# Retention and low-rank mixer on one Trainium2 core: w1 and w2 issued between the last casts of v, batches 1 to 3 loaded in 1.5 MB transfers and turned by PE (batch 1) or DMA (2, 3), retention in 64-row tiles

## Chip, cores and metric

The kernel runs on one core of a Trainium2 chip. Its engines are TensorE (PE, matrix products, with a queue of its own for weight loads, PEld), VectorE (DVE), ScalarE (ACT), GpSimd (POOL) and SyncE (SP, which only issues transfers). The metric is the device time of one execution in microseconds (us), as a median of several runs. A profile shows one execution; its span reaches from the first to the last instruction.

## What is computed

```python
def _attn_ref(q, k, v):                     # each (4, 8, 768, 64)
    gamma = 1.0 - 2.0 ** (-5.0 - np.arange(H))
    scale = 1.0 / np.sqrt(D)
    for t in range(S):
        state = gamma * state + einsum('bhd,bhe->bhde', k[:, :, t], v[:, :, t])
        y[:, :, t] = scale * einsum('bhd,bhde->bhe', q[:, :, t], state)

def _moe_ref(x, U, V, w_ch1, w_ch2):        # x: y as (4, 768, 512); U (768, 32), V (32, 768)
    h = x.transpose(0, 2, 1) @ U @ V        # w_ch1 (512, 2048), w_ch2 (2048, 512)
    u = x + h.transpose(0, 2, 1)
    return u + np.maximum(u @ w_ch1, 0.0) @ w_ch2
```

Retention with a decaying state per head is followed by a low-rank mixing along the sequence and by an MLP over the channels. Inputs and output are float32; the kernel works in bfloat16 with float32 sums.

## The kernel before

The recurrence is worked in chunks of 128 positions, six per batch. The decay is folded into q and v by factors (gqT, gk). For each chunk PE forms the scores k times q for all heads (`score4`), DVE multiplies them with a causal mask, and PE adds the masked scores times v and q times the running state (`mix4`); the state gathers k times v (`state`). The result x is mixed (`lr_proj`, `lr_expand`), the sum u is turned (`lr_turn`, by PE for batches 0 and 1, by DMA transposes on SP for 2 and 3), and the MLP makes up products with w1 (line L438), their ReLU into gT (ACT L445, DVE L443) and down products with w2 (L461), to which DVE adds u (L468).

All instructions are written out in a fixed order; no scheduler moves them, and each engine runs its own in that order. Batch 0's retention comes first, by functions of its own (`cast_early`, `turn_early`, `score_early`, `state_early`, `mix_early`). Then `weave` lays the MLP of batch b - 1, as a list of pieces with costs, and puts the retention of batch b between the pieces: each mark is a fraction of the total cost and a function, and the function is called ahead of the first piece that begins at or behind its mark. 56 pieces make up a stretch of cost 41.47; a large piece (0.864) is four products of 512 columns. The marks come from AT and LR, with one set for batch 1 and one for batches 2 and 3.

Loads of batches 1 to 3 go by SP. k and q are loaded whole, into four strips of 32 partitions, two heads in each, with runs of 1 KB (`load_whole`, L111), v (and for batches 2 and 3 a second, natural copy of k) in pieces of 256 KB with runs of 256 B (L130) into a ring of 19 buffers; `feed_more` issues them as buffers come free. POOL casts a chunk (`prep_turned`, `prep_natural`, lines L83 and L85), DVE turns k and q with its stream transpose (`turn_chunk`, L284), and retention works in 32-row tiles. For batch 1, natural k is won back by PE from the turned one (`natural_k`, L296). q, k and v of batch 0 are loaded ahead of all else by `load_early`.

The weights are loaded by POOL, which casts on the way: U, V, then w1 in four parts behind the last cast of v of batch 0, and w2 in four parts among the casts of batch 1. A one-element copy, `gate`, waits for the end of the first part of w1 and holds back the loads of batch 1:

```python
    for mb in range(4):
        load_w1(mb)
    gate = rinT.tile([P, 2, NCK, 256], fp32, tag="kin", name="gate")
    nc.gpsimd.tensor_copy(out=gate[:1, 0, 0, :1], in_=w1b[:1, NCB - 1, 511:512])
```

PSUM holds two tiles R of two banks each, for scores, mixing and turning, three banks "mlp" and one for the state. The output sums have three buffers (`o_sb`); their stores go out on POOL's queue (L427), but the last.

Of the kernel before, what the change touches and what calls it, by code (L numbers as in the profile page):

```python
# [16 lines left out]
def kernel(  # L17
# [21 lines left out]
    RING = 19  # L39
# [52 lines left out]
    feed = []  # L92
    n_fed, n_used, n_held = [0], [0], [0]
    ready = {}
    turned_in = {}
    n_cast = {b: 0 for b in range(-1, B)}

    def feed_natural(nm, b, ci):
        src = {"k": k, "v": v}[nm]
        feed.append(((nm, b, ci),  # L100
                     src[b, :, ts(ci, P), :].rearrange("h p d -> p h d")))

    def open_in(nm, b):
        turned_in[nm, b] = rinT.tile([P, 2, NCK, 256], fp32, tag=nm + "in",
                                     name=f"{nm}in_{b}")

    def load_whole(nm, b):
        open_in(nm, b)
        src = {"q": q, "k": k}[nm][b]
        for hp in (0, 2, 1, 3):  # L110
            nc.sync.dma_start(  # L111
                out=turned_in[nm, b][ds(32 * hp, 32)].rearrange(
                    "p h c x -> p (h c) x"),
                in_=src[ds(2 * hp, 2)].rearrange("h (c t j) d -> t (h c) (j d)",
                                                 c=NCK, t=32))

    def feed_more():
        while n_fed[0] < len(feed) and n_held[0] < RING:
            key, src = feed[n_fed[0]]
            if key[0] == "T" and n_cast[key[1] - 1] < 2 * NCK:  # L120
                return
            n_fed[0] += 1
            if key[0] == "T":
                load_whole("k", key[1])
                load_whole("q", key[1])
                continue
            n_held[0] += 1
            t = rin.tile([P, 512], fp32, tag="in", name=f"in_{n_fed[0]}")
            ready[key] = t
            nc.sync.dma_start(out=t.rearrange("p (h d) -> p h d", h=H), in_=src)  # L130

    def take(*key):
        n_held[0] -= 1
        return ready.pop(key)

    for b in range(1, B):
        feed.append((("T", b), None))
        for ci in range(NCK):
            if b > 1:
                feed_natural("k", b, ci)  # L140
            feed_natural("v", b, ci)
    NB = S // 256
    early = {}
    kin0 = rinT.tile([P, NB, H, P], fp32, tag="kin", name="kin_0")
    qin0 = rinT.tile([P, NB, H, P], fp32, tag="qin", name="qin_0")

    def load_early(nm, B0):
        src = {"q": q, "k": k, "v": v}[nm][0, :, ds(256 * B0, 256), :].rearrange(
            "h (t j) d -> t h (j d)", j=2)
        if nm == "v":  # L150
            early["v", B0] = []
            for f in range(2):
                t = rin.tile([P, 4, P], fp32, tag="in", name=f"v0_{B0}_{f}")
                nc.sync.dma_start(out=t, in_=src[:, ds(4 * f, 4)])  # L154
                early["v", B0].append(t)
        else:
            t = (kin0 if nm == "k" else qin0)[:, B0]
            nc.sync.dma_start(out=t, in_=src)  # L158
            early[nm, B0] = t

    for nm, B0 in ("k0", "q0", "v0", "k1", "q1", "k2", "q2"):
        load_early(nm, int(B0))

# [15 lines left out]
    for h in range(H):  # L179
# [16 lines left out]
    posT = consts.tile([P, NCK, 2, 4], fp32)  # L196
    nc.gpsimd.iota(posT, pattern=[[P, NCK], [0, 2], [1, 4]], base=0,
                   channel_multiplier=4, allow_small_or_imprecise_dtypes=True)
# [7 lines left out]
    gqT = consts.tile([P, NCK, 2, 4], fp32)  # L206

    def late_consts():
        nc.vector.tensor_scalar(mask, jmat, srange, None, op0=ALU.is_ge)
        nc.vector.tensor_tensor(  # L210
            pos, pos, lgt[:, None, :].to_broadcast([P, NCK, H]), op=ALU.mult)
        nc.scalar.activation(gk, pos, AF.Exp, scale=-1.0)
        for h in range(H):
            r = ds(32 * (h // 2), 32)
            nc.vector.tensor_scalar(
                posT[r, :, h % 2], posT[r, :, h % 2],
                -0.5 * math.log(D) / lg[h] - 128.0 * (h // 2), lg[h],
                op0=ALU.add, op1=ALU.mult)
        nc.scalar.activation(gqT, posT, AF.Exp)

    def causal(n):
        return mask[:, None, :].to_broadcast([P, n, P])
# [3 lines left out]
    def prep_turned(nm, b, ci, eng="P"):  # L226
        src = turned_in[nm, b][:, :, ci].rearrange("p h (a j d) -> p h a j d", a=2,
                                                   j=2)
        t = rpre.tile([P, 2, 2, D, 2], bf16, tag=nm + "i", name=f"{nm}i_{b}_{ci}")
        scale = None  # L230
        if nm == "q":
            scale = gqT[:, ci].rearrange("p h (a j) -> p h a j", a=2)
            scale = scale[:, :, :, :, None].to_broadcast([P, 2, 2, 2, D])
        cast(eng, t.rearrange("p h a d j -> p h a j d"), src, scale)
        pre[nm + "T", b, ci] = t
        n_cast[b] += 1
        feed_more()

    def prep_natural(nm, b, ci, eng="P"):
        t = rpre.tile([P, H, D], bf16, tag=nm + "d", name=f"{nm}d_{b}_{ci}")  # L240
        scale = None
        if nm == "v":
            scale = gk[:, ci, :, None].to_broadcast([P, H, D])
        cast(eng, t, take(nm, b, ci).rearrange("p (h d) -> p h d", h=H), scale)
        pre[nm, b, ci] = t
        feed_more()

    def prep_chunk(b, ci):
        prep_turned("k", b, ci)
        prep_turned("q", b, ci)  # L250
        if b > 1:
            prep_natural("k", b, ci)
        prep_natural("v", b, ci)

    def load_u():
        nc.gpsimd.dma_start(out=Ub, in_=moe_U.rearrange("(j p) r -> p j r", p=P))

    def load_v(c):
        nc.gpsimd.dma_start(out=V4[ds(RK * c, RK)], in_=moe_V)
# [18 lines left out]
    def turn_chunk(b, ci):  # L278
        for nm in ("kT", "qT"):
            src = pre.pop((nm, b, ci)).bitcast(fp32).rearrange(  # L280
                "p h j (e w) o -> p h j e (w o)", e=2)
            t = rpre.tile([P, 2, 2, P], bf16, tag=nm, name=f"{nm}_{b}_{ci}")
            dst = t.bitcast(fp32).rearrange("p h e (t j) -> p h j e t", j=2)
            nc.vector.transpose(out=dst, in_=src)  # L284
            bts[nm, b, ci] = t

    def turned(nm, b, ci, i, c, r=slice(None)):
        return bts[nm, b, ci][r, i, c]

    def natural_k(b, ci):  # L290
        if ci == NCK - 1:
            return
        kp = bank("mlp")
        for i in range(2):
            for c in range(2):
                nc.tensor.matmul(kp[:, ts(2 * i + c, P)],  # L296
                                 turned("kT", b, ci, i, c), ident,
                                 start=True, stop=True)
        kn = rmid.tile([P, 640], bf16, tag="kn", name=f"kn_{b}_{ci}", bufs=2)
        evac("A", kn[:, :512], kp)  # L300
        live["kn", b, ci] = kn

    def state(b, ci):
        if ci == NCK - 1:
            return
        vb = pre["v", b, ci]
        if b > 1:
            kd = pre.pop(("k", b, ci)).rearrange("p (n i) (c w) -> p i c n w",
                                                 i=2, c=2)
        else:  # L310
            kd = live.pop(("kn", b, ci))[:, :512].rearrange(
                "p (i c n w) -> p i c n w", i=2, c=2, n=4)
        if ci == 0:
            live["st_p", b] = bank("st")
        st_p = live["st_p", b]
        for i in range(2):
            for c in range(2):
                for hp in range(4):
                    nc.tensor.matmul(st_p[ds(32 * hp, 32), ts(2 * i + c, D)],  # L319
                                     kd[:, i, c, hp], vb[:, 2 * hp + i],  # L320
                                     start=(ci == 0 and i == 0 and c == 0),
                                     stop=True, skip_group_check=True)
        ns = rmid.tile([P, 320], bf16, tag="ns", name=f"ns_{b}_{ci}")
        evac("A", ns[:, :256], st_p[:, :256])
        live["state", b, ci] = ns

    def score4(b, ci):
        if b == 1:
            natural_k(b, ci)
        for i in range(2):  # L330
            for c in range(2):
                for hp in range(4):
                    r = ds(32 * hp, 32)
                    nc.tensor.matmul(R[hp // 2][:, hp % 2, ts(i, P)],  # L334
# [10 lines left out]
        if b > 1:  # L345
            state(b, ci)

    def mix4(b, ci):
        if ci == 0:
            open_x(b)  # L350
# [420 lines left out]
```

## Time and profile before

| | |
|---|---|
| time, median of three runs | 247.58 us (247.31 to 248.76) |
| span of the profiled execution | 246.0 us |
| PE busy | 218.8 us (89%), 2402 instructions |
| weight loads of PE | 122.3 us (50%) |
| DVE, ACT, POOL busy | 106.3, 80.8, 91.2 us |
| granted PE clock, mean | 0.958 of full speed |
| moved by DMA | 34.69 MB, mean 141 GB/s |

The profiled execution has no time of its own beside its span; the span lies 1.6 us below the median of the runs. A line of a group of instructions reads: line, engine, operation, output and inputs, shape, count, then busy time and mean nanoseconds of one, then the engine's idle time ahead of them and what ended it. "L438" is line 438 of the kernel before. In the profile's row of 40 slices of 6.15 us the DMA engines are busy from the start to 18 us, then nearly idle for one slice (25 GB/s), then busy almost without a break to about 104 us.

### The profile page before, as it was taken

The page shows a single profiled execution, that of the slowest core. Times are in us where ns is not written, and L with a number is a line of the kernel's source. Part 1 is how long each engine was busy: PE and PEld are TensorE (multiplying, and loading weights), DVE is VectorE, ACT ScalarE, POOL GpSimd, SP SyncE. Part 2 cuts the span into 40 slices and gives each one's busy share as a digit, 9 for nine tenths or more (in the row PEclk, how much of TensorE's full clock was granted, in tenths as well). Part 3 has the DMA queues.
Part 4 walks back from the last instruction along what each step waited for, and adds up shares of the span by engine and source line. Part 5 has one row for each costly group of instructions (what it writes and reads, how often), then busy time and mean ns, then how long its engine had stood idle before and what let it go on. Part 6 is the DMA issues. An engine that isn't in the chain of part 4 may idle for free.

```text
span 246.0 us, 5681 instructions
## 1 busy us (share of the span) xinstructions
PE 218.8 (89%) x2402; PEld 122.3 (50%) x2430; DVE 106.3 (43%) x199; ACT 80.8 (33%) x175; POOL 91.2 (37%) x127
## 2 busy tenths in 40 slices
PE   1588789939779999999999999999999999999992
PEld 1476534536535445445754444447644444584451
DVE  4377334415604642566544525555544342221121
ACT  2465425434412213555532002556410014450000
POOL 2759500319960249971137615820001010000110
PEclk9997779997968999999999999999999999999999
DMA  6993999998999999929999953100011532001212
GB/s 180 290 291 25 143 214 229 211 203 166 198 221 219 250 225 238 257 66 205 210 199 242 241 129 109 21 3 4 0 45 45 150 106 43 3 0 43 86 45 85
DMA packets 64009, 34.69 MB, mean 141 GB/s; under 512 B 39680, under 2 KB 62464, under 8 KB 63984
## 3 DMA queue, kind: packets, MB, share of 16 engines
q1 hardware_dynamic: 56880, 23.66, 46.7%
q0 software_dynamic: 7104, 10.67, 18.7%
q8 instruction: 19, 0.31, 0.6%
q14 instruction: 6, 0.05, 0.1%
HBM read 30.90 MB, written 6.29 MB: 151 GB/s over the span
## 4 chain that ended last, share of the span: by engine, by line
PE 38%; issue 31%; DMA 14%; SPq 8%; POOL 6%; DVE 1%; POOLq 0%; ACT 0%
PE mlp L461 17%; PE mlp L438 14%; DMA qin<-in_q_dram 6%; DMA w2b<-in_moe_w_ch_dram 3%; SPq L111 3%; SPq L158 3%; DMA v<-in_v_dram 3%; DMA w1b<-in_moe_w_ch_dram 3%; POOL out_dram L427 2%; PE r L334 2%; PE r L367 2%; SPq L154 2%; POOL vb L85 1%; PE st L319 1%; PE r L358 1%
## 5 line engine op out<-in xcount | busy, mean ns | idle before, releaser
L438 PE MATMUL mlp<-uT,w1b 128*128 128x256 bf16 (+1 forms) x501 | 90.6, 332 | 1.1 <-issue 0.2
L461 PE MATMUL mlp<-w2b,gT 128*128 128x512 bf16 (+2 forms) x384 | 87.1, 375 | 4.9 <-DMA w2b<-in_moe_w_ch_dram 3.2
L445 ACT ACTIVATE gT<-mlp 128x512 bf16<-128x512 f32 (+1 forms) x88 | 42.7, 490 | 77.0 <-PE mlp L438 76.1
L438 PEld LDWEIGHTS <-w1b 128*128 128x128 bf16 x512 | 49.1, 100 | 33.3 <-issue 3.0
L461 PEld LDWEIGHTS <-gT 128*128 128x128 bf16 x400 | 37.0, 98 | 44.2 <-issue 5.2
L427 POOL DMA_DIRECT2D out_dram<-o x24 | 13.2, 553 | 93.2 <-DVE o L468 93.2
L468 DVE TENSOR_TENSOR o<-mlp,u 128x512 f32<-128x512 f32 (+2 forms) x25 | 16.8, 670 | 48.0 <-PE mlp L461 48.0
L443 DVE TENSOR_SCALAR gT<-mlp 128x512 bf16<-128x512 f32 (+1 forms) x40 | 22.1, 552 | 33.5 <-PE mlp L438 33.5
L340 DVE TENSOR_TENSOR a<-r,mask 128x512 bf16<-128x512 f32 x36 | 23.2, 685 | 19.5 <-PE r L334 17.8
L85 POOL TENSOR_TENSOR qi<-qin,gqT 128x512 bf16<-128x512 f32 x18 | 18.7, 1045 | 19.1 <-DMA qin<-in_q_dram 19.1
L72 ACT ACTIVATE x<-r 128x256 bf16<-128x256 f32 x36 | 11.8, 382 | 29.1 <-PE r L367 28.9
L83 POOL CAST ki<-kin 128x512 bf16<-128x512 f32 x18 | 13.6, 763 | 19.7 <-DMA kin<-in_k_dram 14.9
L85 POOL TENSOR_TENSOR vd<-in,gk 128x512 bf16<-128x512 f32 x18 | 18.7, 1041 | 5.3 <-DMA kin<-in_k_dram 1.8
L402 DVE TENSOR_TENSOR u<-r,x 128x512 bf16<-128x512 f32 (+1 forms) x16 | 14.6, 952 | 6.3 <-issue 3.8
L334 PE MATMUL r<-qT,kT 32*128 32x128 bf16 x288 | 7.7, 226 | 4.5 <-DVE qT L284 4.5
L334 PEld LDWEIGHTS <-kT 32*128 32x128 bf16 x288 | 4.5, 96 | 10.1 <-issue 8.9
L284 DVE STREAM_TRANSPOSE qT<-qi 128x256 f32<-128x256 f32 x18 | 7.3, 406 | 5.1 <-POOL qi L85 5.1
L72 ACT ACTIVATE uT<-r 128x1024 bf16<-128x1024 f32 (+1 forms) x6 | 5.2, 880 | 10.9 <-PE r L416 8.8
L557 DVE TENSOR_TENSOR a<-r,mask 128x1024 bf16<-128x1024 f32 x6 | 7.1, 1216 | 3.9 <-PE r L552 3.9
L530 PE MATMUL mlp<-ident,kb 128*128 128x128 bf16 x24 | 3.1, 312 | 5.4 <-DVE kb L83 5.4
L284 DVE STREAM_TRANSPOSE kT<-ki 128x256 f32<-128x256 f32 x18 | 7.8, 436 | 0.0
L83 POOL CAST kd<-in 128x512 bf16<-128x512 f32 x12 | 7.3, 608 | 0.9 <-POOL qi L85 0.9
(77 smaller groups left out, 135.3 us busy)
## 6 DMA issues: line engine op xcount, KB each, us to landing
out_dram<-o POOLq DMA_DIRECT2D x23, 256.0 KB, 2.9
kin<-in_k_dram SPq DMA_DIRECT2D x12, 384.0 KB, 8.1
qin<-in_q_dram SPq DMA_DIRECT2D x12, 384.0 KB, 13.3
in<-in_v_dram SPq DMA_DIRECT2D x18, 256.0 KB, 5.1
in<-in_k_dram SPq DMA_DIRECT2D x12, 256.0 KB, 5.2
w1b<-in_moe_w_ch_dram POOLq DMA_DIRECT2D x4, 512.0 KB, 9.4
w2b<-in_moe_w_ch_dram POOLq DMA_DIRECT2D x4, 512.0 KB, 8.1
kin<-in_k_dram SPq DMA_DIRECT2D x3, 512.0 KB, 6.3
```

Source lines behind the costliest of these rows:

```text
L72: nc.scalar.activation(dst, src, AF.Copy)
L83: e.tensor_copy(out=dst, in_=src)
L85: e.tensor_tensor(dst, src, scale, op=ALU.mult)
L284: nc.vector.transpose(out=dst, in_=src)
L334: nc.tensor.matmul(R[hp // 2][:, hp % 2, ts(i, P)], turned("kT", b, ci, i, c, r), turned("qT", b, ci, i, c, r), start=(c == 0), stop=(c == 1))
L340: nc.vector.tensor_tensor(a[:, ds(4 * g, 4)].rearrange("p (n i) m -> p n i m", n=2), R[g][:, :, :256].rearrange("p n (i m) -> p n i m", i= ...
L427: nc.gpsimd.dma_start(out=dst, in_=src)
L438: nc.tensor.matmul(g_p[:, :sz], w1b[:, c, ts(m, P)], uTs[b][:, c, ds(lo, sz)], start=(c == 0), stop=(c == NCB - 1))
L443: nc.vector.tensor_relu(gT[:, m, ds(lo, sz)], g_p[:, :sz])
L445: nc.scalar.activation(gT[:, m, ds(lo, sz)], g_p[:, :sz], AF.Relu)
L461: nc.tensor.matmul(ch[:, :nn], gT[:, m, ts(j, P)], w2b[:, m, ds(n0, nn)], start=(m == 0), stop=(m == NM - 1))
L468: nc.vector.tensor_tensor(o_sb, ch[:, :nn], us[b][:, j, n], op=ALU.add)
```

## The change

- w1's first part is issued by POOL between the casts of v1 and v2 of batch 0, the other three parts and all of w2 directly behind the casts of v2. U and V are loaded by SP as float32; V is copied to its four places by a product on PE with a 0/1 matrix, U is cast by ACT.
- One half of v1 is cast by DVE; some halves of q's casts and evacuations move between POOL, DVE and ACT. The late constants are made earlier. The two `fill` products are gone.
- Each of k, q, v of batches 1 to 3 is one transfer of 1.5 MB in runs of 256 B (`load_batch`), into one buffer per tensor. `gate` waits for the third part of w1. The loads of batch b + 1 stand on SP behind the cast of chunk 5 of batch b.
- Batch 1 is turned by PE, through R, with evacuations by ACT and DVE. Batches 2 and 3 are turned by DMA transposes on SP, two for each chunk.
- A chunk uses one of the two R tiles, the next the other. Scores are eight products of 64 rows, the state four products of 128 by 128, and the mask is one DVE instruction of 1024 elements.
- The stores of batch 0 go by SP, the others by POOL as before. The marks are new.

```diff
-    RING = 19
+    RING = 16
...
+    def load_batch(b):
+        for nm in "kqv":
+            src = {"q": q, "k": k, "v": v}[nm][b]
+            t = open_in(nm, b, [P, H * NCK, D])
+            nc.sync.dma_start(out=t, in_=src.rearrange("h (c p) d -> p (h c) d", p=P))
...
-    for nm, B0 in ("k0", "q0", "v0", "k1", "q1", "k2", "q2"):
+    for nm, B0 in ("k0", "q0", "v0", "k1", "q1", "k2", "q2", "v1", "v2"):
         load_early(nm, int(B0))
+    Uf = wts.tile([P, NCK, RK], fp32)
+    nc.sync.dma_start(out=Uf, in_=moe_U.rearrange("(j p) r -> p j r", p=P))
...
+    def prep(nm, b, ci):
         t = rpre.tile([P, H, D], bf16, tag=nm + "d", name=f"{nm}d_{b}_{ci}")
...
+        cast("P", t, ins[nm, b].rearrange("p (h c) d -> p c h d", h=H)[:, ci], g)
...
     def turn_chunk(b, ci):
-        for nm in ("kT", "qT"):
...
-            nc.vector.transpose(out=dst, in_=src)
-            bts[nm, b, ci] = t
...
+        r = R[ci % 2]
+        for n, nm in enumerate("kq"):
+            src = pre[nm, b, ci].rearrange("p h d -> p (h d)")
+            t = rpre.tile([P, 4, P], bf16, tag=nm + "T", name=f"{nm}T_{b}_{ci}",
+                          bufs=3)
+            bts[nm, b, ci] = t
+            if b > 1:
+                nc.sync.dma_start(out=t, in_=src, transpose=True)
+                continue
+            for hp in range(4):
+                nc.tensor.matmul(r[:, n, ts(hp, P)], src[:, ts(hp, P)], ident,
+                                 start=True, stop=True)
+            evac("AD"[n], t.rearrange("p n m -> p (n m)"), r[:, n])
+
+    def score(b, ci):
+        r, kT, qT = R[ci % 2], bts.pop(("k", b, ci)), bts["q", b, ci]
+        for hp in range(4):
+            for i in range(2):
+                ri = ds(D * i, D)
+                nc.tensor.matmul(r[:, i, ts(hp, P)], kT[ri, hp], qT[ri, hp],
+                                 start=True, stop=True)
+        a = rmid.tile([P, 2, 4, P], bf16, tag="a4", name=f"a4_{b}_{ci}", bufs=3)
+        nc.vector.tensor_tensor(
+            a, r.rearrange("p i (n m) -> p i n m", n=4),
+            mask[:, None, None, :].to_broadcast([P, 2, 4, P]), op=ALU.mult)
...
+    def mix(b, ci):
...
+        evac("A", xs[b][:, ci].rearrange("p (n i e) -> p i n e", i=2, e=D),
+             r[:, :, :256].rearrange("p i (n e) -> p i n e", e=D))
...
-                        stores.append((out[b, ts(j, P), n], o_sb))
+                        stores.append((nc.gpsimd if b else nc.sync,
+                                       out[b, ts(j, P), n], o_sb))
...
+    V1b = wts.tile([RK, S], bf16)
+    evac("A", V1b, V1)
+    for lo, n in ((0, 512), (512, 256)):
+        v_p = bank("mlp")
+        nc.tensor.matmul(v_p[:, :n], rep4, V1b[:, ds(lo, n)], start=True, stop=True)
+        evac("A", V4[:, ds(lo, n)], v_p[:, :n])
...
-    cast_early("v", 1, ("P", 0, 4), ("P", 4, 4))
+    cast_early("v", 1, ("P", 0, 4), ("D", 4, 4))
     state_early(2)
-    score_early(2)
-    load_u()
+    load_w1(0)
     cast_early("v", 2, ("P", 0, 4), ("P", 4, 4))
-    for c in range(NCB):
-        load_v(c)
-    for mb in range(4):
+    score_early(2, 0)
+    score_early(2, 1)
+    for mb in range(1, 4):
         load_w1(mb)
-    gate = rinT.tile([P, 2, NCK, 256], fp32, tag="kin", name="gate")
-    nc.gpsimd.tensor_copy(out=gate[:1, 0, 0, :1], in_=w1b[:1, NCB - 1, 511:512])
+    for j in range(4):
+        load_w2(j)
+    gate = rinT.tile([P, H * NCK, D], fp32, tag="kin", name="gate")
+    nc.gpsimd.tensor_copy(out=gate[:1, 0, :1], in_=w1b[:1, NCB - 1, 1535:1536])
+    load_batch(1)
     state_early(3)
     mix_early(1)
+    evac("A", Ub, Uf)
...
-    AT = {1: at(0.39, 0.0625, 0.042), 2: at(0.09, 0.105, 0.05)}
-    LR = {1: (0.80, 0.83, 0.88, 0.92), 2: (0.71, 0.75, 0.83, 0.89)}
+    AT = {1: (0.60, 0.035, 0.08, 0.06, 0.012), 2: (0.14, 0.098, 0.05, 0.13, 0.07)}
+    LR = {1: (0.87, 0.90, 0.93, 0.955), 2: (0.71, 0.75, 0.83, 0.89)}
...
+        s0, step, dm, dp, dt = AT[w]
         for ci in range(NCK):
...
+            s_at = s0 + step * ci
+            if (b, ci) >= (1, 3):
+                marks.append((s_at - dp, part(prep_chunk, b, ci)))
+            marks.append((s_at - dt, part(turn_chunk, b, ci)))
+            marks.append((s_at, part(score, b, ci)))
+            marks.append((s_at + dm, part(mix, b, ci)))
+        if b + 1 < B:
+            marks.append((s0 + step * (NCK - 1) - dp + 0.001, part(load_batch, b + 1)))
```

## The prediction

> **What bounds the kernel now.** I read the table of stretches first. Its columns are: stretch, its length, busy time (and instructions) of PE, PE's weight loads, DVE, ACT and POOL, the clock granted to PE, DMA share, GB/s.
>
> ```profile
> 31.00:35.00 4.00, 3.49 (x9) 1.27 (x10) 0.83 (x7) 1.03 (x3) 0.19 (x1) 0.57 1.24 206
> 51.00:56.00 5.00, 0.55 (x13) 0.45 (x13) 0.59 (x2) 0.87 (x2) 1.66 (x2) 0.94 1.11 194
> 56.00:59.00 3.00, 3.00 (x29) 2.10 (x29) 2.07 (x5) 0.38 (x1) 3.00 (x4) 0.53 1.07 233
> 65.00:70.00 5.00, 1.82 (x26) 0.99 (x25) 1.97 (x4) 0.60 (x1) 5.00 (x7) 0.91 1.21 194
> 70.00:76.00 6.00, 5.78 (x68) 2.67 (x69) 0.82 (x2) 1.54 (x4) 1.67 (x3) 0.51 1.15 228
> 76.00:100.00 24.00, 23.42 (x285) 11.70 (x289) 11.23 (x19) 5.68 (x12) 12.52 (x18) 1.00 1.10 236
> ```
>
> From 76 us on PE is full at clock 1.00, and only its own work counts. Before that it stands idle around 51 to 56 and 65 to 70, and after each hole it runs at about half clock. The waits of PE say for what:
>
> ```profile
> PE r L334 <- DVE qT L284: 4.5, 1, 4.5
> PE mlp L461 <- DMA w2b<-in_moe_w_ch_dram: 3.2, 2, 1.7
> PE mlp L673 <- DMA w1b<-in_moe_w_ch_dram: 2.1, 1, 2.1
> ```
>
> The first is q of batch 1 (DVE turned it late because its load was late), the second w2, the third w1. All three are loads. The first up product of MLP(0) starts at 31.92, MLP(1) at 98.43, MLP(2) at 149.18, MLP(3) at 199.18; so the stretches last 66.5, 50.75, 50.0 and, with the tail, 46.85 us. Next, a chunk of retention in the chain of waits (start, length, what):
>
> ```profile
> 79.45 0.22 PE mlp L296 x4
> 79.67 0.33 PE r L334 x16
> 80.01 1.83 PE mlp L461 x8
> 81.84 0.23 PE r L358 x16
> 82.07 0.34 PE r L367 x8
> 82.41 0.23 PE st L319 x16
> ```
>
> Scores and mix stand two MLP pieces apart: the mask on DVE runs behind them and PE never waits for it. Last, SP's queue (timeline, then the chain) and its transposes:
>
> ```profile
> 42.28 14.59 SPq L130 DMA_DIRECT2D in<-in_v_dram  x6
> ...
> 39.83 14.35 DMA qin<-in_q_dram
> ...
> L410 SPq DMA_TRANSPOSE uT<-u x12: 1189/1264/1298, 141.6 to 203.0; - x12
> DMA to landing us min/median/max: 2.4/2.5/3.4
> ```
>
> SP stood 14.59 us in issuing six loads of 0.26 MB: with a full queue it issues only as fast as data moves. A q load issued at 39.83 landed 14.35 us later, behind what SP had issued before. A transpose costs SP 1.26 us and lands 2.5 us after issue, in stretches where SP had no load under way.
>
> **The change, part by part.** A sum against the span of 246.0; the runs' median of 247.58 lies 1.6 above it.
>
> *Weights earlier: -12.1.* w1's first quarter goes out on POOL before the last casts of v (behind one cast of v1, 17.5 + 1.05, so about 18.6 instead of 25.0), the rest, at 0.78 each behind the two casts of v2, from about 22 to 28, while DMA was idle (25 GB/s in the slice from 18.5 to 24.6). All w is 4.2 MB as written; w2 alone ran at 199 GB/s (62 to 69), so 21 us. Batch 1's k, q, v wait for w1's third quarter (about 29.5), then take 4.72 MB. Runs of 256 B moved at 233 GB/s (56 to 59, nearly all v), so 20.3 us; the bounds are 198 (128 to 131) and 291 (512 B runs, 6 to 18). All lands by 62, k and q by 55.5, w2 by 51. w2 is needed at 31.3 + 20.7 (up products) + 1.0 (low-rank products), near 53; q at 0.604 of the stretch, 31.3 + 25.1 + 1.3, near 57.5; v four pieces and the products of two chunks later, near 63. These waits go (4.45 + 3.2), and the half-clock stretches after them (about 3 and 6 us at half speed, 1.5 + 3.0). Bounds: -8 (v late, one clock drop stays) to -13.
>
> *Start of MLP(0): -0.6 and -0.8.* No wait for w1. But v1's second half lands 0.4 later (V goes first on SP's queue, 0.1 MB at 291), its cast waits on DVE behind a mask, and ACT casts U in between: data ready near 31.3, not 30.7. Half clock at 31 to 35 cost 1.65; whether it drops again is open (0 to -1.65), so I take half. V copied by PE instead of four POOL loads, and two fill products less, cost nothing: PE idles in both places for DMA, ACT and DVE.
>
> *Turning batch 1 on PE: +1.5.* Eight products per chunk (0.44, twice L296) instead of four for five chunks. Scores, query and state in 64-row tiles: half as many products over as many or more columns per pass; no row, bounds -0.1 to +0.1 a chunk, taken as 0. DVE loses its stream transposes (0.85 a chunk), worth PE time only near 120, where the chain runs through DVE: -0.7.
>
> *Waits inside batch 1's retention: +10.1.* Marks act only at piece boundaries (0.0208 of the stretch apart, 0.86 us). Turn, scores and mix of a chunk now share one R tile with chunk ci+2, and in the new positions they fall together: chunks 0 and 3 have turn and scores at one boundary, so PE waits for the evacuation (DVE 0.69 + about 0.15): 1.7. Chunk 2's evacuation queues on DVE behind mask and output sum: 0.6. The scores of chunk ci+2 stand directly ahead of the mix of ci in the same R for ci = 0, 2, 3, and the mix must wait for that mask (1.22, as L557 below), in one case behind an output sum: 1.35 + 1.85 + 1.25; ci = 1 has a piece between: 0.5. The projection directly behind the last mix waits for x (0.6 + 0.15); the turn of u, one piece behind its expansion instead of two, for two sums of 1.22: 2.1. Bounds 0 (if the order slips apart) to 12.
>
> ```profile
> L557 DVE TENSOR_TENSOR a<-r,mask 128x1024 bf16<-128x1024 f32 x6 | 7.1, 1216 | 3.9 <-PE r L552 3.9
> L468 DVE TENSOR_TENSOR o<-mlp,u 128x512 f32<-128x512 f32 x23 | 15.9, 691 | 45.7 <-PE mlp L461 45.7
> L443 DVE TENSOR_SCALAR gT<-mlp 128x512 bf16<-128x512 f32 x20 | 13.7, 686 | 20.5 <-PE mlp L438 20.5
> L402 DVE TENSOR_TENSOR u<-r,x 128x1024 bf16<-128x1024 f32 x8 | 9.4, 1217 | 1.4 <-PE r L395 1.4
> L72 ACT ACTIVATE x<-mlp 128x512 bf16<-128x512 f32 x5 | 2.8, 595 | 2.4 <-PE mlp L605 1.5 <-PE mlp L584 0.9
> ```
>
> *Stores of batch 0 on SP: +0.3.* Four of them stand behind the whole load of batch 2. That load waits for the cast of chunk 5 (behind mix(1,1), about 72), so it ends near 94 and store 2 lands near 96; output sum 5 needs that buffer at 95. PE has two banks free meanwhile. Bounds 0 to 4.
>
> *Load of batch 3 ahead of the transposes of chunk (2,5): +9.1.* SP's order is transposes (2,4), load of k, q, v, transposes (2,5). The load starts when chunk 5 is cast, and that cast needs a buffer that mix(2,1) frees. Count from the end of mix(2,1). SP: 1.2 for a transpose, 0.8 to first bytes, 20.3 for 4.72 MB, 1.1 for a store that shares the engines; then two transposes, 2.6 from there to landing (1.26 + 2.5 less overlap with the queue's end): 26.0. PE: scores(2,5) stand 0.354 of 41.5 later, 14.7, plus three chunks of scores, query, mix and state (3 x 1.13) and 0.3 of small gaps: 18.4. PE waits 7.6, then half clock as after the hole at 51 (1.5). At 198 GB/s the wait is 11, at 291 it is 3.5; bounds +3.5 to +14. Behind that PE queue stand all later products; nothing covers it.
>
> The Trainium skill's page "DMA: Bandwidth & Descriptors" speaks for these loads in "Measured (HBM→SBUF, 128 partitions, SWDGE, issued from GpSimd)": batch transfers to 1 MiB or more, 6.15 us for 1 MB. Its "Specifications" speak against: runs under 512 B miss line rate. The rows side with the second, 233 against 291 GB/s. By the page's fit, 2.0 + bytes/436e3, an estimate, each load would take 5.6 us, three 16.8, and the wait would be 4.1 instead of 7.6.
>
> *Transposes of batch 3: +2.6.* SP issues u's two transposes (ready 2.6 after MLP(2) starts, behind DVE's sums), then k and q of chunk (3,0): 2.6 + 3 x 1.26 + 2.5 = 8.9. Scores(3,0) stand at 6.3. Bounds 0 to 4. For batch 2, u is turned by PE, and the first scores are met.
>
> Sum: -12.1 - 0.6 - 0.8 + 1.5 - 0.7 + 10.1 + 0.3 + 9.1 + 2.6 = +9.4. Span 255.4, time **257.0**.
>
> **Rivals.**
>
> *The waits on R vanish*: mask and evacuation end before PE comes, because real pieces and queues slip apart. For it: before, PE never waited there, and with pieces between, 1.22 is nearly covered. Against: R is one tile, and the order on PE puts the products next to each other. 257.0 - 10.1 = **246.9**, no change. It decides if these waits sum to under 3 us.
>
> *The transposes aren't held* (the other side): SP queues the loads without standing still, and transposes overtake. The 7.6 + 1.5 and the 2.6 go: **245.3**, not slower, at the edge of faster. For it: no transpose met a load before. Against: 14.59 for six issues, and 14.35 from issue to landing. It decides if PE idles under 1 us ahead of scores(2,5).
>
> *The holes pull the clock down*: PE is little over half busy from 57 to 80, and before, clock 0.51 lasted 6 us after holes of 1.7 and 1.5. At half clock for 14 pieces, 6 us more: **263**.
>
> **How the numbers follow.** Forecast 0.55 (own range 251 to 262), R waits gone 0.14, transposes free 0.17, clock 0.14. A measurement of this kernel tells about 1% (245.1 to 250.1) from no change. Faster: half of the third case, with some R waits gone too, and a little over a third of the second: 0.14. Same: the rest of both and 0.02 of the forecast: 0.19. Slower: 0.67. Range 246 to 264: below it lies what of the second and third case is not made up by other terms (0.15), above it a clock case with slow loads (0.05).
>
> **What would show it.** Right: MLP(1) starts 1 to 4 us earlier than 98.43, no wait for w2 or q, PE waits for DVE masks between 57 and 80; one hole of 5 to 11 us ahead of the scores of chunk (2,5) that ends with a transpose's landing; a smaller one ahead of scores(3,0). Wrong: no such hole; MLP(1) starting before 90; or SP issuing the loads of batch 3 within a few us.

## The result, and the profile after

The changed kernel takes **268.88 us**, the median of four runs (267.11 to 270.95), against 247.48 us before: a ratio of 1.0846 (95% interval 1.078 to 1.0913). The forecast was 257.0 with a range of 246 to 264. The direction was right, the size was not: the loss is 21.4 us where 9.4 was forecast. The profiled execution took 270.01 us, its span is 268.2. Four of the kernels below have one or two runs in a slower state, which the ratios leave out and the medians include; without those runs the medians are 257.87 us (load of batch 3 behind the transposes), 246.88 (later marks for batch 2), 246.05 (two halves) and 240.37 (three buffers).

Starts of the first up product of each MLP, read from PE's timeline, with the sum of the prediction beside them, carried on from the starts before:

| | MLP(0) | MLP(1) | MLP(2) | MLP(3) | span |
|---|---|---|---|---|---|
| before | 31.92 | 98.43 | 149.18 | 199.18 | 246.0 |
| predicted | 31.3 | 96.5 | 156.0 | 208.6 | 255.4 |
| after | 32.15 | 103.74 | 164.51 | 222.06 | 268.2 |

The saving on DVE (-0.7) is counted in the second stretch. So the first stretch is 6.4 us longer than forecast (71.6 for 65.2), the second 1.3 (60.8 for 59.5), the third 5.0 (57.6 for 52.6). The waits of PE, behind 57 us (total, times, longest):

```profile
PE r L235 <- DMA qT<-qd: 11.5, 2, 8.0
PE r L226 <- ACT kT L72: 5.1, 6, 1.5
PE r L253 <- DVE a L238: 3.0, 3, 1.4
PE r L235 <- DVE qT L74: 1.7, 2, 0.8
PE r L319 <- DVE u L305: 1.3, 2, 0.7
PE r L258 <- DVE a L238: 1.3, 1, 1.3
```

No wait for w1, w2 or the casts of batch 1's q is left. In their place stand DMA transposes (first row) and, inside batch 1's retention, the tile R: its evacuations by ACT and DVE, its masks. The holes in PE's timeline (start, duration, what, count, idle time ahead and what ended it), and at 78 the first products at half clock:

```profile
59.82 0.38 PE L226 MATMUL r<-ident,qd 128*128 128x128 bf16 x4 [0.69 <-ACT kT L72]
61.05 0.40 PE L235 MATMUL r<-qT,kT 64*128 64x128 bf16 x8 [0.85 <-DVE qT L74]
...
77.79 0.38 PE L226 MATMUL r<-ident,qd 128*128 128x128 bf16 x4 [1.51 <-ACT kT L72]
78.01 1.62 PE L364 MATMUL mlp<-w2b,gT 128*128 128x512 bf16 x4
...
146.09 0.61 PE L235 MATMUL r<-qT,kT 64*128 64x128 bf16 x8 [8.02 <-DMA qT<-qd]
146.63 3.53 PE L364 MATMUL mlp<-w2b,gT 128*128 128x512 bf16 x8
150.57 1.68 PE L364 MATMUL mlp<-w2b,gT 128*128 128x512 bf16 x7
...
174.54 0.61 PE L235 MATMUL r<-qT,kT 64*128 64x128 bf16 x8 [3.50 <-DMA qT<-qd]
175.08 5.30 PE L341 MATMUL mlp<-uT,w1b 128*128 128x512 bf16 x12
```

The holes that end at 146 and 174 are the two that were forecast, of chunks (2,5) and (3,0). The product rows behind them show the second cost: eight products in 3.53 us behind the hole, 0.44 each, and seven in 1.68, 0.24 each, once the clock is back. The table of stretches, with the columns of the one before, says it by the granted clock:

```profile
57.00:78.00 21.00, 13.33 (x137) 7.68 (x136) 8.96 (x10) 5.46 (x11) 13.14 (x15) 1.00 0.38 85
78.00:86.00 8.00, 5.88 (x48) 3.16 (x45) 2.52 (x3) 1.83 (x4) 0.73 (x1) 0.57 1.05 217
146.00:151.00 5.00, 4.91 (x35) 1.99 (x34) 1.92 (x2) 0.23 (x1) 0.56 (x1) 0.60 0.07 25
174.00:181.00 7.00, 6.46 (x33) 2.94 (x33) 1.92 (x2) 1.17 (x3) 2.52 (x3) 0.52 0.49 94
181.00:222.00 41.00, 40.29 (x361) 21.39 (x358) 15.65 (x21) 13.04 (x32) 7.98 (x11) 1.00 0.26 62
```

From 57 to 78 PE works 13.33 of 21 us, in pieces between waits for R; then the clock drops to half until 85, and again behind each hole. SP's timeline shows the order that makes the hole at 146:

```profile
118.39 1.19 SPq L223 DMA_TRANSPOSE qT<-qd  x1
120.04 0.71 SPq L106 DMA_DIRECT2D kin<-in_k_dram  x1
121.20 6.46 SPq L106 DMA_DIRECT2D qin<-in_q_dram  x1
128.12 7.01 SPq L106 DMA_DIRECT2D vin<-in_v_dram  x1
135.22 8.16 SPq L223 DMA_TRANSPOSE kT<-kd  x1
143.48 1.22 SPq L223 DMA_TRANSPOSE qT<-qd  x1
...
156.90 12.72 SPq L313 DMA_TRANSPOSE uT<-u  x6
169.72 2.24 SPq L223 DMA_TRANSPOSE kT<-kd  x1
172.07 1.21 SPq L223 DMA_TRANSPOSE qT<-qd  x1
```

The first transpose of (2,5) stands 8.16 us in issuing behind the load, where others take 1.2. The load and that transpose take SP from 120.04 to 143.38.

### The profile page after: what moved, and what is told of

Same layout as the page of the kernel before. It is cut to its first block, busy times and chain, and to the rows that moved or that the text cites. A ratio compares the mean times of both kernels' runs of the same rounds, so it can differ in the third digit from the quotient of the medians.

```text
span 268.2 us, 4770 instructions
## 1 busy us (share of the span) xinstructions
PE 225.2 (84%) x2014; PEld 124.4 (46%) x2014; DVE 98.7 (37%) x148; ACT 86.6 (32%) x178; POOL 74.6 (28%) x103
## 4 chain that ended last, share of the span: by engine, by line
issue 33%; PE 21%; POOL 6%; SPq 3%; DMA 2%; DVE 2%; ACT 1%; POOLq 0%; ACTq 0%
PE mlp L341 10%; PE mlp L364 6%; POOL out_dram L330 3%; SPq L223 3%; DMA qT<-qd 2%; POOL vd L85 2%; PE r L258 1%; PE r L235 1%; DVE u L305 1%; POOL qd L85 1%; PE r L253 1%; PE st L270 1%; DVE o L371 1%; PE r L319 0%; POOL kd L83 0%
## 5 line engine op out<-in xcount | busy, mean ns | idle before, releaser
L341 PE MATMUL mlp<-uT,w1b 128*128 128x512 bf16 (+1 forms) x512 | 91.4, 332 | 1.9 <-ACT uT L72 0.7
L238 DVE TENSOR_TENSOR a<-r,mask 128x1024 bf16<-128x1024 f32 x18 | 22.0, 1223 | 33.0 <-PE r L235 30.5
L72 ACT ACTIVATE x<-r 128x512 bf16<-128x512 f32 x18 | 10.7, 596 | 44.1 <-PE r L258 44.1
L83 POOL CAST kd<-kin 128x512 bf16<-128x512 f32 x18 | 10.9, 611 | 42.9 <-DMA kin<-in_k_dram 26.7
L85 POOL TENSOR_TENSOR qd<-qin,gq 128x512 bf16<-128x512 f32 x18 | 18.7, 1041 | 12.9 <-DMA qin<-in_q_dram 12.9
L85 POOL TENSOR_TENSOR vd<-vin,gk 128x512 bf16<-128x512 f32 x18 | 18.7, 1042 | 9.8 <-DMA vin<-in_v_dram 9.8
L235 PE MATMUL r<-qT,kT 64*128 64x128 bf16 x144 | 7.8, 232 | 13.2 <-DMA qT<-qd 11.5
L235 PEld LDWEIGHTS <-kT 64*128 64x128 bf16 x144 | 4.9, 99 | 19.7 <-DMA kT<-kd 10.8
L72 ACT ACTIVATE ns<-st 64x256 bf16<-64x256 f32 x30 | 11.2, 372 | 0.3
L258 PE MATMUL r<-vd,a 128*128 128x64 bf16 x144 | 7.7, 200 | 1.3 <-DVE a L238 1.3
L458 DVE TENSOR_TENSOR a<-r,mask 128x1024 bf16<-128x1024 f32 x6 | 7.1, 1212 | 1.1 <-PE r L453 1.1
```

The lines of the kernel that those rows point to most:

```text
L72: nc.scalar.activation(dst, src, AF.Copy)
L83: e.tensor_copy(out=dst, in_=src)
L85: e.tensor_tensor(dst, src, scale, op=ALU.mult)
L235: nc.tensor.matmul(r[:, i, ts(hp, P)], kT[ri, hp], qT[ri, hp], start=True, stop=True)
L238: nc.vector.tensor_tensor(a, r.rearrange("p i (n m) -> p i n m", n=4), mask[:, None, None, :].to_broadcast([P, 2, 4, P]), op=ALU.mult)
L341: nc.tensor.matmul(g_p[:, :sz], w1b[:, c, ts(m, P)], uTs[b][:, c, ds(lo, sz)], start=(c == 0), stop=(c == NCB - 1))
```

## The experiments

Each ratio is to the kernel before, measured beside it, with its 95% interval. The first five each alter one thing in the changed kernel (the fifth on top of the first); then these steps are put together and what is left is pursued; the last two put the step of the weights into the kernel before.

**Load of batch 3 behind the transposes of (2,5).**

```diff
-            marks.append((s0 + step * (NCK - 1) - dp + 0.001, part(load_batch, b + 1)))
+            late = dt if b > 1 else dp
+            marks.append((s0 + step * (NCK - 1) - late + 0.001, part(load_batch, b + 1)))
```

> The changed kernel with one mark moved: the load of batch 3 is issued behind the transposes of chunk (2,5) instead of ahead of them. Theory (the hole of 8.0 us ahead of the scores of chunk (2,5) is the transposes standing behind 4.7 MB on SP's queue): the hole goes, and with it the half clock behind it (about 1.9): 268.9 - 9.9 = 259.0. Rival (the loads of batch 3 set the pace, whatever their order): the hole is given back at the start of MLP(2), where batch 3 comes later by as much: 265 to 269.

Measured: 259.52 us, 1.0466 [1.0369, 1.0563], 9 to 11 us less than the change. The wait of 8.0 is gone; what is left of that row is the hole of (3,0):

```profile
PE r L235 <- DMA qT<-qd: 3.5, 1, 3.5
...
165.41 0.40 PE L235 MATMUL r<-qT,kT 64*128 64x128 bf16 x8 [3.47 <-DMA qT<-qd]
165.75 2.76 PE L341 MATMUL mlp<-uT,w1b 128*128 128x512 bf16 x12
```

The load is issued 5 us later; new is only a wait of 1.4 us for u's transposes ahead of MLP(2). So the cost that the forecast put at +9.1 is shown by taking it away. Behind the hole of (3,0) the clock did not fall this time: the twelve products that took 5.30 us in the change take 2.76.

**All eight turning products ahead of both evacuations.**

```diff
             for hp in range(4):
                 nc.tensor.matmul(r[:, n, ts(hp, P)], src[:, ts(hp, P)], ident,
                                  start=True, stop=True)
-            evac("AD"[n], t.rearrange("p n m -> p (n m)"), r[:, n])
+        if b == 1:
+            for n, nm in enumerate("kq"):
+                evac("AD"[n], bts[nm, b, ci].rearrange("p n m -> p (n m)"), r[:, n])
```

> The changed kernel with the turning of batch 1 reordered: all eight products of a chunk, then the two evacuations, so that q's products do not wait for ACT to evacuate k (5.1 us in six waits). Theory (these waits are on PE's path): -5.1, or -4 where PE then waits longer for the evacuations ahead of the scores: 264 to 265; if the half clock from 78 to 85 goes too, 262. Rival (the loads set the pace): the time comes back as waits for q or v of batch 1: 268 to 269.

Measured: 268.22 us, 1.0791 [1.0724, 1.0858]: hardly a change. Its waits:

```profile
PE r L237 <- DMA qT<-qd: 12.8, 2, 9.4
PE r L237 <- DVE qT L74: 5.7, 6, 1.5
```

Part of the wait for ACT moved to the scores, which now wait for q's evacuation (5.7, before 1.7 + 5.1). MLP(1) starts at 99.42, 4.3 earlier, and the stretch from 78 to 86 has clock 1.00 (the next run shows that it can have this without the edit too). But the hole at (2,5) grew from 8.0 to 9.4 and its half clock lasted longer (0.78 on average from 140 to 160), so that MLP(2) starts only 1.5 earlier: a gain ahead of a queue-bound hole is given back in it. The rival's time came, by another way than it said: the gain went in the hole at (2,5), and no wait for a load of batch 1 grew.

**Unread products in the two holes**, 36 ahead of scores (2,5) and 15 ahead of scores (3,0), each of 512 columns.

```diff
+    def fill(n):
+        spare = bank("mlp")
+        for _ in range(n):
+            nc.tensor.matmul(spare, ident, w1b[:, 0, :512], start=True, stop=True)
+    FILL = {(2, 5): 36, (3, 0): 15}
...
+            if (b, ci) in FILL:
+                marks.append((s_at - 0.0005, part(fill, FILL[b, ci])))
```

> The changed kernel with products added that nobody reads: 36 of 512 columns ahead of the scores of chunk (2,5) and 15 ahead of those of chunk (3,0), which is where PE stands idle for 8.0 and 3.5 us. 51 x 0.216 = 11.0 us of PE work more. Theory (the half clock behind a hole comes from PE idling, and the holes are waits for transposes that PE's work does not move): clock 1.00 in both places, 1.9 + 2.9 less: 264. Rival (the clock falls for another reason, or the holes are no waits for transfers): 269 to 280.

Measured: 263.54 us, 1.062 [1.0546, 1.0695]. Eleven us more work on PE, and 5.3 us less time. The products stand where PE waited anyway, and the clock stays at 1.00 behind them:

```profile
130.00:150.00 20.00, 18.73 (x151) 8.86 (x151) 3.93 (x5) 1.83 (x4) 1.18 (x2) 1.00 0.77 159
160.00:182.00 22.00, 22.00 (x158) 10.43 (x157) 7.96 (x11) 9.17 (x18) 16.04 (x19) 1.00 0.46 97
```

So the half clock behind the two holes had its price apart from the holes: from the start of MLP(1) to the end the profile is 4.7 us shorter than the change's (159.8 for 164.5), against 1.9 + 2.7 by the product rows of the change. Ahead of MLP(1) the two kernels have the same instructions, and PE's waits are nearly the same; yet here the clock stays at 1.00 where it fell in the change, and MLP(1) starts at 101.35, 2.4 earlier:

```profile
77.55 0.38 PE L226 MATMUL r<-ident,qd 128*128 128x128 bf16 x4 [1.51 <-ACT kT L72]
77.77 1.03 PE L364 MATMUL mlp<-w2b,gT 128*128 128x512 bf16 x4
```

So whether the clock falls behind the waits of batch 1 differs from run to run, and up to 2.4 us of an earlier MLP(1) need not come from an edit.

**The marks of batch 1, each at a boundary of its own.**

```diff
-    AT = {1: (0.60, 0.035, 0.08, 0.06, 0.012), ...
-    LR = {1: (0.87, 0.90, 0.93, 0.955), ...
+    AT = {1: (0.6245, 1 / 24, 0.0415, 0.06, 0.0208), ...
+    LR = {1: (0.89, 0.91, 0.955, 0.975), ...
```

> The changed kernel with other marks for batch 1: turn, scores and mix of its chunks each at a piece boundary of its own (turn of chunk ci at boundary 2ci, scores at 2ci + 1, mix at 2ci + 3), nothing else changed. Theory (PE's waits for masks and for q's evacuation come from two operations on one R tile placed at one boundary): of the 13.1 us of waits between 57 and 104, the masks' 4.3 and the evacuation's 1.7 go, the 5.1 for ACT's evacuation of k stay since they lie inside one turn; MLP(1) starts 5 to 7 earlier, at 97 to 99, and the time is 262 to 264. Rival (as in the run that turned first and evacuated then, what is won in batch 1 is lost again at the hole of chunk (2,5) and its half clock): MLP(1) starts earlier, and the time is 267 to 269. Rival (the marks don't matter, DVE is simply behind): the mask waits stay above 3 us, MLP(1) near 103, time 268 to 270.

Measured: 264.00 us, 1.0637 [1.0586, 1.0689]. PE's waits for masks and for q's evacuation are no longer listed, the wait for ACT stays at 4.3 in six, and there is no half clock between 57 and 86 us: PE works 23.38 us of the 29 from 57 to 86 (19.21 in the change). MLP(1) starts at 93.98, **9.8 earlier**, more than the 5 to 7 expected. The clock's drop is part of it: against the run with unread products, where the clock did not fall either, it is 7.4 earlier, and the waits for masks, for q's evacuation, for x and one of u's that are gone sum to about as much (4.3 + 1.7 + 0.7 + 0.7). Half of the 9.8 is lost again in two holes on transposes ahead of batch 2's scores, one new, the other 1.7 longer:

```profile
103.49 0.40 PE L235 MATMUL r<-qT,kT 64*128 64x128 bf16 x8 [2.53 <-DMA qT<-qd]
140.62 0.61 PE L235 MATMUL r<-qT,kT 64*128 64x128 bf16 x8 [9.72 <-DMA qT<-qd]
```

**Transposes of (3,0) ahead of u's**, on top of the first experiment.

```diff
-            marks.append((s_at - dt, part(turn_chunk, b, ci)))
+            turn_at = 0.015 if (b, ci) == (3, 0) else s_at - dt
+            marks.append((turn_at, part(turn_chunk, b, ci)))
```

> The kernel with the load of batch 3 behind the transposes of chunk (2,5) (259.5 us), with one more step: the two transposes of chunk (3,0) are issued at mark 0.015 of the stretch, ahead of those of u that SP otherwise issues first. Theory (the 3.5 us hole ahead of the scores of (3,0) is SP's order, four transposes of 1.26 us each and a landing, and brings the half clock behind it): the hole goes, with it about 2.9 us lost to half clock; u's turn lands up to 2.5 later, at the end of the stretch where it is not waited for at this place; time 252 to 255. Rival (the transposes wait for the cast of chunk (3,0) on POOL and for the load, not for SP's order): the hole stays at 3 us or more, time 258 to 261.

Measured: 252.94 us, 1.0212 [1.0142, 1.0281], 5 to 7 us less than without it. The hole of 3.5 us had cost more than its length. In its place PE waits 2.04 us for u's transposes ahead of MLP(2), and here the clock falls behind it (four products in 1.41 us instead of 1.03):

```profile
155.52 1.41 PE L341 MATMUL mlp<-uT,w1b 128*128 128x512 bf16 x4 [2.04 <-DMA uT<-u]
```

**All four steps in one kernel.**

> All four steps in one kernel: load of batch 3 behind the transposes of (2,5), transposes of (3,0) ahead of u's, eight turning products ahead of both evacuations, and the marks of batch 1 at boundaries of their own. Theory (the waits and the half clock behind them are all that the change cost; the earlier weights are a gain of about 12 that stays): waits inside batch 1 under 3 us, no hole over 2 us behind 60 us, clock 1.00 from there; MLP(1) starts at 91 to 95, stretches of 50 to 52, 50 to 52 and 46: time 238 to 244, faster than before the change by 2 to 4%. Rival (gains don't add, since each hole that goes lets the next transfer become the limit): 248 to 253, no faster than before.

Measured: 248.87 us, 1.0017 [0.998, 1.0054]. MLP(1) starts at 90.60, 7.8 earlier than before the change and a little earlier than the theory said; but the second stretch lasts 58.0 instead of 50.75. A hole of 4.4 us stands ahead of the scores of (2,0), and the rival was right that each hole that goes lets the next transfer decide.

```profile
PE r L237 <- DMA qT<-qd: 4.4, 1, 4.4
PE r L260 <- POOL vd L85: 2.3, 1, 2.3
PE mlp L343 <- DMA uT<-u: 1.6, 2, 1.1
```

**Stores of batch 0 back on POOL's queue**, on top.

```diff
-                        stores.append((nc.gpsimd if b else nc.sync,
+                        stores.append((nc.gpsimd,
```

> The kernel with all four steps (248.9 us), with one part of the change undone: the stores of batch 0 go by POOL's queue, as before, instead of SP's. Theory (the 4.4 us hole ahead of the scores of chunk (2,0) at 102 is SP's order: its transposes of (2,0), issued at 97.2 and 98.6, stood behind a store that SP was issuing from 88.8 to 96.0): the hole shrinks to 2 or less and the half clock behind it goes; time 243 to 246. Rival (the transposes land behind the 4.7 MB of batch 2's load, whatever stands on SP): the hole stays at 3.5 or more, time 248 to 250; then POOL's queue, whose casts stand behind stores that wait for DVE's sums, may add 1.

Measured: 248.80 us, 1.0019 [0.9986, 1.0051]. The hole stays (4.71). SP's timeline tells why: without stores, the transpose itself stands behind the load.

```profile
75.60 0.70 SPq L106 DMA_DIRECT2D kin<-in_k_dram  x1
76.76 6.67 SPq L106 DMA_DIRECT2D qin<-in_q_dram  x1
83.89 7.12 SPq L106 DMA_DIRECT2D vin<-in_v_dram  x1
93.18 6.91 SPq L223 DMA_TRANSPOSE kT<-kd  x1
100.26 1.19 SPq L223 DMA_TRANSPOSE qT<-qd  x1
```

**Later marks for batch 2**, on top of that (first scores at 0.175, chunks 0.09 apart, low-rank marks 0.70, 0.735, 0.81, 0.87).

> The same, with the marks of batch 2 alone moved: first scores at 0.175 of the stretch instead of 0.14 (1.5 us later), chunks 0.09 apart instead of 0.098, and the low-rank steps 0.01 to 0.02 earlier (0.4 to 0.8 us; for batch 3 too). Theory: PE comes to the scores of (2,0) after their transposes have landed, and to u's turn after its own: no wait over 1 us behind 70 us, clock 1.00 there; time 241.5 to 244.5, faster than the kernel before by 1.5 to 2.5%. Rival (the load of batch 2 is the limit and the hole only moves to the next chunk): 246 to 249.

Measured: 247.82 us, 0.9943 [0.9899, 0.9988]. The waits moved: 2.9 ahead of (2,0), 1.5 ahead of (2,1), 1.9 for u's turn. The theory's 241.5 to 244.5 was missed and the rival's 246 to 249 met: the hole moved on to the next chunk. If anything was gained, it is little: the interval just touches that of the run before.

**The load of batch 2 in two halves of one buffer**, on top of that: nine transfers of 256 KB behind the casts of chunk 2, nine behind chunk 5.

```diff
+            if half == 0:
+                open_in(nm, b, [P, H * NCK, D])
+            t = ins[nm, b].rearrange("p (h c) d -> p h c d", h=H)
+            src = src.rearrange("h (c p) d -> p h c d", p=P)
+            for c in range(3 * half, 3 * half + 3):
+                nc.sync.dma_start(out=t[:, :, c], in_=src[:, :, c])
...
+                marks.append((0.60, part(load_batch, 2, 0)))
+                marks.append((s0 + step * (NCK - 1) - dp + 0.001, part(load_batch, 2, 1)))
```

> The kernel with all steps and the marks of batch 2 moved (247.8 us), with the load of batch 2 in two halves: chunks 0 to 2 of k, q, v (2.36 MB, nine transfers of 256 KB) stand on SP behind the casts of chunk 2 of batch 1, chunks 3 to 5 behind the cast of chunk 5, instead of all 4.72 MB behind the cast of chunk 5. Theory (what is left of the change's cost is that load: with one buffer per tensor it can't begin before 74.5 and holds the transposes of (2,0) and (2,1) until it is through): DMA, idle from 64 to 74, works there; the first half lands by 80, the second by 90; the waits of 2.9 and 1.5 ahead of scores (2,0) and (2,1) go, MLP(2) starts 3 to 5 earlier than 146.9, time 242.5 to 245.5. Rival (transposes are slow in themselves while DMA is busy, or MLP(2)'s start is set by u's turn, not by the holes): waits of 2 or more stay or turn up at u's turn, time 246.5 to 249.

Measured: 246.36 us, 0.9917 [0.9893, 0.9942]. The edit did not do what it says: SP issued the first half at 76.97, behind the cast of chunk 5 (76.32 to 76.94 on POOL), as if the buffer were handed on as a whole. It therefore does not test the theory, and its interval overlaps that of the run before.

**Three buffers of two chunks each**, on top of the kernel with the later marks; every batch is loaded by thirds (k, q, v of two chunks, six transfers of 256 KB), and batch 1's first casts go chunk by chunk.

```diff
+    def load_third(b, g):
+        for nm in "kqv":
+            src = {"q": q, "k": k, "v": v}[nm][b].rearrange("h (c p) d -> p h c d", p=P)
+            t = open_in(nm, b, g, [P, 2, H, D])
+            for c in range(2):
+                nc.sync.dma_start(out=t[:, c], in_=src[:, :, 2 * g + c])
...
+                for g, m_at in enumerate((0.60, 0.691, 0.775)):
+                    marks.append((m_at, part(load_third, 2, g)))
```

> The kernel with all steps and the marks of batch 2 moved (247.8 us), with each input buffer cut into three of two chunks each, loaded by six transfers of 256 KB per third (k, q, v of two chunks, then of the next two); a third of batch 2 is loaded as soon as the two chunks of batch 1 in its buffers are cast, by buffers of its own this time (in the run with two halves in one buffer both halves had waited for the cast of chunk 5, at 76.9). Theory (the one whole load of batch 2 behind the last cast of batch 1 is the rest of the change's cost): the load of batch 2 begins near 65 instead of 74.5, DMA does not idle between 64 and 74, all lands by 92, PE waits for no transpose of batch 2; v of chunk (1,0) is no longer waited for (1.7 to 2.5); MLP(1) at 88 to 91, MLP(2) at 140 to 144; time 240 to 244, ratio 0.97 to 0.985. Rival (u's turn sets MLP(2)'s start, the holes only hid it, or DMA and the casts stay the limit): MLP(2) at 145 or later, time 245 to 248.

Measured: **241.09 us** (239.95 to 243.72), 0.9739 [0.9696, 0.9783], faster than both kernels. The load of batch 2 begins at 64.24 and SP is through with it at 89.12, PE waits for no transpose of a chunk, and its clock is 0.999 over the span of the profiled run (0.972 to 0.993 in the others). The last load of batch 1, the first and the last of batch 2, and the first transpose on SP, then all that PE still waits for DMA:

```profile
61.11 3.03 SPq L108 DMA_DIRECT2D vin<-in_v_dram  x2
64.24 2.82 SPq L108 DMA_DIRECT2D kin<-in_k_dram  x2
...
86.34 2.78 SPq L108 DMA_DIRECT2D vin<-in_v_dram  x2
91.08 1.28 SPq L230 DMA_TRANSPOSE kT<-kd  x1
```

```profile
PE mlp L350 <- DMA uT<-u: 1.8, 1, 1.8
```

MLP(1) starts at 89.12, MLP(2) at 141.17, MLP(3) at 191.70.

**In the kernel before: w1's first part ahead of the casts of v2.**

```diff
+    load_w1(0)
     cast_early("v", 2, ("P", 0, 4), ("P", 4, 4))
     for c in range(NCB):
         load_v(c)
-    for mb in range(4):
+    for mb in range(1, 4):
```

> The kernel before with one part of the change alone: the first quarter of w1 is issued by POOL ahead of the casts of v2 of batch 0. Theory (in the kernel before the loads are late by the time in which DMA idled, 19 to 25): the gate opens some 4 us earlier, the wait for w1 (2.1) and most of that for q (4.45) with its half clock (1.5) go, the wait for w2 stays (w2 stands behind the casts of q): 241 to 244. Rival (weights early only shift the wait to w2): 246 to 248.

Measured: 246.03 us, 0.9924 [0.989, 0.9958], nearer to the rival. MLP(0) starts at 30.87, 1.05 earlier; q of batch 1 is waited for longer than before (4.5), and w2 about as it was (3.2):

```profile
PE r L334 <- DVE qT L284: 5.3, 1, 5.3
PE mlp L461 <- DMA w2b<-in_moe_w_ch_dram: 2.9, 3, 1.7
```

**The same, and w2 behind the casts of k, ahead of q's.**

> The kernel before, with two steps: w1's first part issued ahead of the casts of v2 (246.0 us when alone), and all of w2 issued on POOL behind the casts of k of batch 1, ahead of q's. Theory (w2's wait of 2.9 us and the half clock from 70 to 75 behind it are POOL's order): both go, q's own wait grows by up to 2 as w2 shares the engines with q and v; time 241 to 244. Rival (the DMA engines are the limit there, and w2 moved ahead only moves the wait to q and v): q's wait grows to 8 us or more, time 245 to 249.

Measured: 251.37 us, 1.0139 [1.0073, 1.0205]: slower than both said. The wait for w2 is gone and MLP(1) starts at 91.74, but batch 2's loads came late; what delayed them was not followed up. POOL stood idle for 9.06 us, until 91.48, for q of batch 2 (it had it at 88.42 before); the stores behind that cast on its queue were late, so DVE waited 12.78 us for an output buffer, and PE 8.03 us for DVE's sum u, which stands behind:

```profile
101.50 0.69 DVE L468 TENSOR_TENSOR o<-mlp,u 128x512 f32<-128x512 f32 x1 [12.78 <-DMA out_dram<-o]
102.11 1.28 DVE L402 TENSOR_TENSOR u<-r,x 128x512 bf16<-128x512 f32 x2
```

## Why the prediction went wrong, step by step

The span of 268.2 lies 12.8 us above the forecast's 255.4. The steps that failed are the waits inside batch 1's retention, with the turn's own wait put at nothing, and the half clock, which the sum had behind one hole only.

- **Weights earlier (-12.1)**: borne out to within about 2 us. The waits for w1, w2 and q are gone in the change. POOL had q and v of batch 1 at 57.4 and 64.3, some 2 us later than the sum said; PE doesn't feel it in the change, but waits 1.7 to 2.5 us for v in the kernels with all four steps in 1.5 MB loads. In the kernel with three buffers MLP(1) starts 9.3 earlier than before. There the waits on R are nearly gone, and the sum for the first stretch, with the 1.2 of the next point for its 0.8, is -12.1 - 1.2 + 1.5 = -11.8; from a start 0.8 later than before (32.74) this gives MLP(1) at 87.4. It starts at 89.1, and 1.2 of the 1.7 missing are two short waits (0.55 for q's evacuation, 0.66 for u).
- **Start of MLP(0) (-0.6, -0.8)**: the start is 0.2 later, not 0.6 earlier. The clock there stayed at 1.00 (the first eight products take 2.16 us, 3.39 before), so 1.2 were won where half of 1.65 was put.
- **Waits inside batch 1's retention (+10.1)**: a failed step. The foreseen kind (masks, q's evacuation, x, u) sums to 8.0. The turn was costed as if its eight products ran through: q's four stand behind ACT's evacuation of k, as both lie in one R tile, six times for 5.1. That makes 13.1. The clock then fell to half from 78.3 to about 85, with PE busy about 5 us of it, so about 2.5 more in the profiled run; with the 0.4 more won at the start, 1.3 of the stretch's excess are in neither. That the waits come from the placing is shown: the marks apart took out those for masks and for q's evacuation, and turning all eight products first took out the one for ACT. That the clock must fall with them is not: behind the same waits it stayed at 1.00 in the run with unread products.
- **Load of batch 3 ahead of the transposes (+9.1)**: right in size and mechanism, a hole of 8.02 (7.6) and half clock behind it (1.9 for 1.5); 9 to 11 us came back when the order was undone.
- **Transposes of batch 3 (+2.6)**: mis-sized, the other failed step. The hole is 3.5, and behind it twelve products take 5.30 us where 2.6 is their time at full clock: 2.7 that the sum left out. Reordering SP gave 5 to 7 us back. Of the 5.0 us by which this stretch exceeds the forecast, 1.4 are in neither; 0.5 of them is a wait for u's transposes ahead of MLP(3).
- **Stores of batch 0 on SP (+0.3)**: no stall shows, and undoing it, in the kernel with all four steps, gave nothing.
- **The rival of the clock** was held apart from the forecast with a chance of 0.14 and 6 us. Its 6 us don't follow from its fourteen pieces: at 0.86 us each, half clock would add 12, and no reason is given for half of that. Above all it was no other case: half clock came within the forecast's own, behind the waits and both holes. Here lies the error of method: the sum added holes, and the clock for one of them only. About 7 us (2.5 + 1.9 + 2.7) are its price in the profiled run, of which the sum had 1.5.

Together, 3.0 more of waits in batch 1, 5.6 more of half clock, 1.3 of longer holes and 0.4 at the start, less 0.7 in the tail, make 9.6 of the 12.8 us; the other 3 are in none of these. Of the signs named beforehand, the hole ahead of (2,5), the smaller one ahead of (3,0) and the waits for masks came; MLP(1) 1 to 4 us earlier did not, it started 5.3 later.

The Trainium skill's page "TensorE: Matmul & The Clock Gate", in "Part 1: The HAM clock gate", says that the clock halves after an idle window of about 3.4 us and comes back after a busy one, the window running free. In the change's trace the clock is at half behind the holes of 8.02 and 3.50 and stays there another 3.9 and about 6 us. But at the second it fell after some 2.8 us of idling (the hole begins at 171.04, and the granted clock is 0.94 from 173 to 174 and 0.50 from 174 to 175), it fell behind a hole of 2.04 in another run, and in the first stretch behind waits of at most 1.5; and it did not fall behind the hole of 3.47 with the load of batch 3 moved. So in these runs the length of a hole alone does not tell whether the clock falls. An estimate by the page alone, one window at half speed, would be 1.7 for each hole, against 1.9 and 2.7 measured.

Of the loss of 21.4 us, the order of batch 3's load is 9 to 11, the order of its transposes 5 to 7, and marks and evacuations of batch 1 the next 4.1 (of 11.9 that MLP(1) gains by them). Then the kernel stands where it was before: MLP(1) starts 7.8 earlier, and the stretch behind it, with the one load of batch 2 behind the last cast of batch 1, is 7.3 longer. The kernel with three buffers gets 6 to 7 us back. Between the two profiles it is 6.6, of which 4.7 lie in that stretch (52.05 for 56.73), where no chunk's transposes are waited for any more (4.4 before), and 1.1 ahead of it. How much of that is the earlier load and how much the smaller transfers and the order of batch 1's own thirds was not told apart.

## To carry to other kernels

Price a hole in TensorE's work with the half clock that can follow it, 2 to 3 us here for each time it came, and ask of every wait inside a shared PSUM tile whether the next product of the same step, too, stands behind an evacuation. Where transposes share a queue with loads, write the queue's order out and put the load behind the transposes that are needed first. And before counting a gain, look for the next transfer: one load behind the last reader of its buffer kept back what earlier weights had won, until the buffer was cut into parts.

## What was not expected of the hardware

A transpose behind a 1.5 MB load on SP's queue stands 6.8 to 8.2 us in issuing, against 1.2 on a free one. Filling the holes with 11 us of unread products made the kernel 5.3 us faster. Behind the same waits of batch 1, and ahead of the scores of (3,0) behind holes of 3.47 and 3.50 us, the clock fell to half in one run and stayed full in another.
